# Attention and snake MLP on one core: the fourth chunk scaled by VectorE and transposed on TensorE, the fifth scaled in quarters, the last values interleaved, alpha spread later

## Chip, cores, metric

One core of a Trainium2 chip. The metric is the device time of one execution in microseconds (us). Every execution quoted is of the state "fast"; as will be seen, that state still holds several levels.

## The reference

```python
# q, k, v: (8, 12, 448, 64); w_in: (768, 2048); w_out: (2048, 768); float32
q_n, k_n = rmsnorm(q, g_q), rmsnorm(k, g_k)            # over the 64 of a head
attn = softmax(q_n @ k_n.T / 8)                         # per batch and head
x = (attn @ v), heads side by side                      # (3584, 768)
h = x @ w_in
g = h + sin(alpha * h)**2 / alpha
out = g @ w_out
```

## The kernel before

Eight batches, one after the other. Each has an attention stage and then its first product, h(b). The second product of a batch fills the gaps of the next batch's attention stage. In the first attention stage there is no such product, so TensorE runs dummy matmuls instead. q and k come in chunks of four heads, three chunks to a batch, numbered from 0: "fourth chunk" is number 3. Chunks 0 to 2 ("early") are scaled by VectorE (DVE) and transposed on TensorE (for chunk 1, 28 transposes of 64x64 take 0.89 us there, and the copies after them 1.16 us on DVE). The later ones are scaled by GpSimd (POOL) and transposed by DMA. Names in the profile: sc are scores, expT their exponentials, qkn scaled q and k, qkT the same transposed, av the values' products, hps the sums of h, g_sb the result of the snake function, osb the output before it is stored. What the change touches:

```python
def bank_pair(name, dtype=F32):          # PSUM: four pairs of banks; the pair expected
    slot = min(free_at, key=free_at.get) # to be free first is taken
    ...
early = ci < NC                          # NC = 3 chunks of a batch
def scale(w):
    eng = nc.vector if early else nc.gpsimd
    ...                                  # two multiplications of 128x448
def spread_alpha():                      # alpha to one column per tile
    ps = bank_pair("aps")
    nc.tensor.matmul(ps[:, 0, :MT], small, ident_f32, start=True, stop=True)
    nc.vector.tensor_copy(alpha_sb[:, :, 0], ps[:, 0, :MT])
    ...
# snake: who squares the sine
if m % 2 == 0 and (b or m <= MT // 2):
    nc.gpsimd.tensor_mul(s2, s1, s1)
else:
    nc.scalar.activation(s2, s1, ACT.Square)
...
# stage one: S_(n) is a tile of scores with n dummies ahead, A_ the values of a head pair
c0.pe_transpose((0, 1), (0,))
spread_alpha()
c1.reduce(0), c1.reduce(1)
S_(), S_()
c1.rsqrt()
S_(3)
c1.scale(0), c1.scale(1)
load_qk(NC)
S_(3), S_(2), S_(2), S_(1)
...                                      # chunks 1 and 2, loads of weights and v
A_(), S_(1), S_(1), S_(1)
c2.pe_transpose((0, 1))
S_(2), A_(), S_(2)
step_of(NC, 3, 4)()                      # chunk 3: sums of squares
S_(2), S_(1), A_()
step_of(NC, 5, 6)()                      # chunk 3: scale on GpSimd, DMA transposes, load chunk 6
load_w_out(1)
S_(1), S_(1), A_(), S_()
step_of(NC + 1, 3, 4)()
S_(), A_(2)                              # A_(2): pairs 4 and 5, key tiles 0 to 5, then tile 6
c4.rsqrt()                               # chunk 4: g folded, scaled and transposed beside h(0)
first_product(0, beside)
```

## Time and profile before

| | before |
|---|---|
| median of 3 runs | 439.59 us (438.88 to 439.76) |
| the profiled run, one more | 440.08 us, span 438.3 us |
| TensorE busy | 423.9 us (97%) |
| h(0) begins | 39.56 us |
| h(1) begins | 92.72 us |

The prediction shows the lines that carry the reading. After 83 us TensorE never waits, so as far as TensorE sets the time only the first 83 us can change it.

### The profile page before, as it was taken

To read this page: it belongs to the slowest core of one execution; us is meant where nothing else is said; L and a number is where in the kernel's file an instruction comes from. 1 tells how busy PE (TensorE), PEld (TensorE's weight loads), DVE (VectorE), ACT (ScalarE), POOL (GpSimd) and SP (SyncE) were. 2 spreads that over 40 slices of the span, in tenths; PEclk is the share of its full clock that TensorE was granted. 3 is DMA by queue.
4 is the path that set the end of the run, shared out by engine and by line. 5 is a ranking of instruction groups with operands and counts; after the bars stand their busy time and mean duration, and the time that the engine had idled before them with its cause. 6 is when DMAs were issued, how large, how long until landed. Compare 5 with 4: busy or idle time off the path is not lost.

```text
span 438.3 us, 9452 instructions
## 1 busy us (share of the span) xinstructions
PE 423.9 (97%) x3817; PEld 220.3 (50%) x3819; DVE 227.5 (52%) x329; ACT 340.0 (78%) x532; POOL 280.5 (64%) x264
## 2 busy tenths in 40 slices
PE   7889988999999999999999999999999999999996
PEld 3434543555555555555555554555555555555563
DVE  4767463547454574455636574555635474246511
ACT  5888897878888788878888788887878788788600
POOL 4969869917797469937699269956599276003300
PEclk9999999999999999999999999999999999999999
DMA  7999999790067804593076903596063901320022
GB/s 252 210 255 189 188 214 243 226 231 6 20 181 194 176 2 94 152 211 114 2 199 167 204 0 50 167 214 141 2 179 100 125 0 28 90 56 0 1 72 73
DMA packets 70096, 55.09 MB, mean 126 GB/s; under 512 B 41492, under 2 KB 65828, under 8 KB 70052
## 3 DMA queue, kind: packets, MB, share of 16 engines
q1 hardware_dynamic: 56690, 40.97, 36.9%
q0 software_dynamic: 12416, 11.81, 18.0%
q10 hardware_dynamic: 946, 1.70, 1.0%
q8 instruction: 30, 0.49, 0.4%
q14 instruction: 14, 0.11, 0.1%
HBM read 45.62 MB, written 11.01 MB: 129 GB/s over the span
## 4 chain that ended last, share of the span: by engine, by line
PE 83%; ACT 4%; DMA 4%; POOL 4%; DVE 2%; issue 2%; POOLq 0%; ACTq 0%
PE ops L400 31%; PE hps L353 30%; PE av L314 13%; PE sc L294 8%; DMA qkT<-qkn 3%; POOL qk L224 2%; ACT expT L297 2%; ACT s L332 1%; DMA qk<-in_k_dram 1%; POOL sq L221 1%; DVE ms L227 1%; DVE xT L326 1%; ACT s L337 1%; POOL vb L135 1%; DVE qkn L246 0%
## 5 line engine op out<-in xcount | busy, mean ns | idle before, releaser
L297 ACT ACTIVATE expT<-sc 128x896 bf16<-128x896 f32 x168 | 144.5, 912 | 31.9 <-PE sc L294 31.2
L400 PE MATMUL ops<-w_out_sb,g_sb 128*128 128x384 bf16 x896 | 156.7, 327 | 0.0
L353 PE MATMUL hps<-xT,w_in 128*128 128x448 bf16 x768 | 146.7, 353 | 0.0
L335 POOL TENSOR_TENSOR s<-s 128x448 f32<-128x448 f32 x61 | 56.7, 934 | 114.6 <-ACT s L332 100.4
L400 PEld LDWEIGHTS <-g_sb 128*128 128x128 bf16 x896 | 83.1, 98 | 69.5 <-issue 18.4
L340 DVE SCALAR_TENSOR_TENSOR g_sb<-s,inv_alpha_sb,hps 128x448 bf16<-128x448 f32 x128 | 80.8, 676 | 63.3 <-POOL s L335 62.3
L353 PEld LDWEIGHTS <-w_in 128*128 128x128 bf16 x768 | 74.5, 98 | 71.5 <-issue 2.9
L326 DVE TENSOR_TENSOR xT<-av,rec 64x448 bf16<-64x448 f32 x96 | 59.7, 622 | 70.6 <-ACT rec L321 51.5
L332 ACT ACTIVATE s<-hps,alpha_sb 128x448 f32<-128x448 f32 x128 | 74.9, 627 | 26.7 <-PE hps L353 23.9
L246 POOL TENSOR_TENSOR qkn<-qk,inv 128x448 bf16<-128x448 f32 x84 | 76.2, 940 | 10.0 <-POOL qk L224 6.0
L221 POOL TENSOR_TENSOR sq<-qk 128x896 f32<-128x896 f32 x44 | 73.4, 1686 | 0.0
L314 PE MATMUL av<-expT,vb 64*64 64x448 bf16 x672 | 69.2, 349 | 1.8 <-ACT expT L297 0.9
L314 PE MATMUL av<-expT,ones 64*64 64x448 bf16 x672 | 69.2, 349 | 0.0
L294 PE MATMUL sc<-qkT 64*64 64x448 bf16 x672 | 51.8, 361 | 4.4 <-DMA qkT<-qkn 1.8
L227 DVE TENSOR_REDUCE ms<-sq 128x14 f32<-128x896 f32 x44 | 46.8, 1081 | 16.3 <-POOL sq L221 16.1
L406 DVE COPY osb<-ops 128x768 f32<-128x768 f32 (+1 forms) x33 | 27.6, 837 | 46.7 <-PE ops L400 40.1
L224 POOL TENSOR_TENSOR qk<-qk,gg 128x896 f32<-128x896 f32 x24 | 50.2, 2091 | 1.8 <-ACT gg L171 1.7
L314 PEld LDWEIGHTS <-vb 64*64 64x64 bf16 x672 | 37.6, 107 | 14.0 <-issue 2.6
L314 PEld LDWEIGHTS <-ones 64*64 64x64 bf16 x672 | 37.1, 107 | 11.6
L337 ACT ACTIVATE s<-s 128x448 f32<-128x448 f32 x67 | 38.6, 577 | 3.5 <-DVE g_sb L340 0.5
L294 PEld LDWEIGHTS <-qkT 64*64 64x64 bf16 x672 | 15.3, 104 | 34.4 <-issue 28.5
L320 ACT ACTIVATE rec<-av 128x448 f32<-128x448 f32 x48 | 26.1, 544 | 3.7 <-PE av L314 3.2
(44 smaller groups left out, 136.6 us busy)
## 6 DMA issues: line engine op xcount, KB each, us to landing
qk<-in_q_dram SPq DMA_DIRECT2D x24, 448.0 KB, 5.5
qk<-in_k_dram SPq DMA_DIRECT2D x22, 448.0 KB, 5.9
out_dram<-osb SPq DMA_DIRECT2D x39, 192.0 KB, 2.8
vb<-in_v_dram POOLq DMA_DIRECT2D x32, 168.0 KB, 6.6
w_in<-in_moe_w_in_dram POOLq DMA_DIRECT2D x4, 768.0 KB, 11.0
w_out_sb<-in_moe_w_out_dram POOLq DMA_DIRECT2D x2, 1536.0 KB, 25.2
out_dram<-osb SPq DMA_DIRECT2D x26, 96.0 KB, 6.2
qk<-in_k_dram ACTq DMA_DIRECT2D x2, 448.0 KB, 6.0
```

The costliest lines, as they stand in the source:

```text
L221: nc.gpsimd.tensor_mul(st.sq[w], qk[ci][:, w], qk[ci][:, w])
L224: eng.tensor_mul(qk[ci][:, 0], qk[ci][:, 0], gg.to_broadcast([P, 2 * NJ, D]))
L246: eng.tensor_mul(n[:, :, hi, :], x[:, hi], inv[:, hi].unsqueeze(2).to_broadcast([P, NJ, D]))
L294: nc.tensor.matmul(sc[key_rows(pp, hi), pp, :S], qkt[r, 1, j * REST:(j + 1) * REST], qkt[r, 0, :], start=True, stop=True)
L297: nc.scalar.activation(expT[c, j], sc[:, :, :S], ACT.Exp, scale=SCALE)
L314: nc.tensor.matmul(av[o, part, :S], ones[r, :] if part else vb[b][r, hp, j, :], expT[pi // 2, j][r, pi % 2, :], start=(j == 0), stop=(j == ...
L326: nc.vector.tensor_mul(xT[b][r, hp, :], av[r, 0, :S], rec[o, :])
L332: nc.scalar.activation(s1, hps, ACT.Sin, scale=alpha_sb[:, m, :])
L335: nc.gpsimd.tensor_mul(s2, s1, s1)
L340: nc.vector.scalar_tensor_tensor(g_sb[:, m, (b % 2) * S:(b % 2 + 1) * S], s2, inv_alpha_sb[:, m, :], hps, op0=ALU.mult, op1=ALU.add)
L353: nc.tensor.matmul(ps[:, m % 2, :S], w_in_sb[m * 2 // MT][:, kt, m % (MT // 2) * P:(m % (MT // 2) + 1) * P], x[:, kt, :], start=(kt == 0), ...
L400: nc.tensor.matmul(st["ps"][:, k, :HALF], g_sb[:, m, c0:c0 + P], w_out_sb[:, m, half * HALF:(half + 1) * HALF], start=(m == 0), stop=(m == ...
```

## The change

Its intent: in the first stage GpSimd and the DMA queue are the late ones (chunk 4's transposes arrive near 72 us, and TensorE waits for them), while VectorE has time. So chunk 3 goes to VectorE and TensorE; chunk 4's folding of g moves up into the place set free on GpSimd; its scaling is cut in quarters between the squares of h(0), which all go to GpSimd; and the last two pairs' values are taken key tile by key tile, to use the wait for the last exponentials. Besides, alpha's matmul and copy move behind chunk 1's scaling, and chunk 6 and the second half of w_out are loaded earlier.

```diff
-        early = ci < NC
+        early = ci <= NC
-            for hi in range(2):
+            for hi in heads:                       # scale(w, heads=(0, 1))
...
-        if m % 2 == 0 and (b or m <= MT // 2):
+        if m % 2 == 0:
...
     c0.pe_transpose((0, 1), (0,))
-    spread_alpha()
...
-            for js in (range(NJ - 1), [NJ - 1]):
+            for j in range(NJ):
                 for pi in list(pairs)[:n]:
-                    attend(pi, js)
+                    attend(pi, [j])
...
     c1.scale(0), c1.scale(1)
+    spread_alpha()
     load_qk(NC)
...
+    load_w_out(1)
+    c4.fold_g()
     A_(), S_(1), S_(1), S_(1)
     c2.pe_transpose((0, 1))
-    S_(2), A_(), S_(2)
-    step_of(NC, 3, 4)()
-    S_(2), S_(1), A_()
-    step_of(NC, 5, 6)()
-    load_w_out(1)
+    S_()
+    c3.reduce(0), c3.reduce(1)
+    A_(), S_(2)
+    c3.rsqrt()
+    S_(2)
+    c3.scale(0), c3.scale(1)
+    load_qk(NC + 3)
+    S_(1), A_()
+    c3.pe_transpose((0, 1))
     S_(1), S_(1), A_(), S_()
...
-    for i, task in ((2, c4.fold_g), (4, lambda: c4.scale(0)), (5, lambda: c4.scale(1)), (6, step_of(NC + 1, 6))):
+    for i, task in ((2, lambda: c4.scale(0, [0])), (3, lambda: c4.scale(0, [1])), (4, lambda: c4.scale(1, [0])),
+                    (5, lambda: c4.scale(1, [1])), (6, step_of(NC + 1, 6)), (6, beside[3].pop())):
```

More of the change, by code (lines that the diff above doesn't have):

```diff
@@ L237, in rsqrt, with scale @@
             nc.scalar.activation(inv[:, ws, :2 * NJ], ln[:, ws], ACT.Exp, scale=-0.5)
-        def scale(w):
+        def scale(w, heads=(0, 1)):
             eng = nc.vector if early else nc.gpsimd
@@ L244, in scale @@
             inv = st.inv[w].rearrange("p (hi j) -> p hi j", hi=2)
-            for hi in range(2):
+            for hi in heads:
                 eng.tensor_mul(n[:, :, hi, :], x[:, hi], inv[:, hi].unsqueeze(2).to_broadcast([P, NJ, D]))
-            st.scaled += 1
-            if st.scaled == 2:
+            st.scaled += len(heads)
+            if st.scaled == 4:
                 for ps, time in st.inv_ps:
@@ L499 @@
     begin_norm(NC)
-    step_of(NC, 0, 1, 2)()
+    c3 = norm[NC]
+    c3.square(0), c3.square(1)
+    c3.fold_g()
     nc.gpsimd.tensor_copy(gate, qk[NC + 1][:, 1, 0, 0:1])
@@ L504 @@
     begin_norm(NC + 1)
-    step_of(NC + 1, 0, 1)()
+    c4 = norm[NC + 1]
+    c4.square(0), c4.square(1)
     for part in load_v(1):
         part()
+    load_w_out(1)
+    c4.fold_g()
     A_(), S_(1), S_(1), S_(1)
     c2.pe_transpose((0, 1))
-    S_(2), A_(), S_(2)
-    step_of(NC, 3, 4)()
-    S_(2), S_(1), A_()
-    step_of(NC, 5, 6)()
-    load_w_out(1)
+    S_()
[7 more added lines that the diff above has]
+    c3.pe_transpose((0, 1))
     S_(1), S_(1), A_(), S_()
-    step_of(NC + 1, 3, 4)()
+    c4.reduce(0), c4.reduce(1)
     S_(), A_(2)
-    c4 = norm[NC + 1]
     c4.rsqrt()
     beside = beside_h(0)
-    for i, task in ((2, c4.fold_g), (4, lambda: c4.scale(0)), (5, lambda: c4.scale(1)), (6, step_of(NC + 1, 6))):
+    for i, task in ((2, lambda: c4.scale(0, [0])), (3, lambda: c4.scale(0, [1])), (4, lambda: c4.scale(1, [0])),
+                    (5, lambda: c4.scale(1, [1])), (6, step_of(NC + 1, 6)), (6, beside[3].pop())):
         beside.setdefault(i, []).append(task)
```

## The prediction

> **What bounds the kernel now.** I read the busy strip first, then TensorE's waits in two windows, then the timelines of the first 95 us engine by engine. Three rows of the strip (40 slices of 11 us; tenths of busy time):
>
> ```profile
> PE   7889988999999999999999999999999999999996
> ACT  5888897878888788878888788887878788788600
> POOL 4969869917797469937699269956599276003300
> ```
>
> After the first eight slices TensorE is the bound. TensorE's waits say it exactly. From 0 to 40 us, and from 40 us to the end:
>
> ```profile
> PE sc L290 <- ACT expT L297: 1.2, 2, 1.1
> PE sc L294 <- DVE qkT L276: 1.0, 3, 0.7
> PE av L314 <- ACT expT L297: 0.9, 2, 0.7
> ...
> PE sc L294 <- DMA qkT<-qkn: 1.8, 2, 1.4
> PE sc L294 <- ACT expT L297: 1.0, 1, 1.0
> PE av L314 <- DVE osb L406: 0.9, 1, 0.9
> PE sc L294 <- DVE g_sb L340: 0.3, 1, 0.3
> ```
>
> The columns are total us, times, longest. The last four rows are all that TensorE loses after 40 us, 4.0 us of 398. TensorE's timeline gives their places, all between h(0) and the end of the second attention stage:
>
> ```profile
> 60.10 0.38 PE L294 MATMUL sc<-qkT 64*64 64x448 bf16 x4 [0.27 <-DVE g_sb L340]
> 63.88 0.38 PE L294 MATMUL sc<-qkT 64*64 64x448 bf16 x4 [1.03 <-ACT expT L297]
> 70.18 0.38 PE L294 MATMUL sc<-qkT 64*64 64x448 bf16 x2 [0.37 <-DMA qkT<-qkn]
> 71.97 0.76 PE L294 MATMUL sc<-qkT 64*64 64x448 bf16 x10 [1.41 <-DMA qkT<-qkn]
> 82.48 0.38 PE L314 MATMUL av<-expT,vb 64*64 64x448 bf16 x2 [0.90 <-DVE osb L406]
> ```
>
> From 83 us on it waits for nothing, so every microsecond won or lost before that point reaches the end unchanged, and nothing else can. The first stage (0 to 39.56 us, where h(0) starts) is different: TensorE there is padded with dummy matmuls and goes in step with ScalarE's exponentials, DVE and four PSUM bank pairs. ScalarE's and DVE's rows there:
>
> ```profile
> 14.58 0.32 ACT L236 ACTIVATE inv<-ms,eps 128x28 f32<-128x28 f32 x1
> 15.06 4.13 ACT L297 ACTIVATE expT<-sc 128x896 bf16<-128x896 f32 x5
> 20.04 2.53 ACT L297 ACTIVATE expT<-sc 128x896 bf16<-128x896 f32 x3 [0.85 <-PE sc L294]
> 15.22 2.22 DVE L246 TENSOR_TENSOR qkn<-qk,inv 128x448 bf16<-128x448 f32 x4 [0.67 <-POOL gate L444]
> 18.41 1.16 DVE L276 COPY qkT<-tp 128x896 bf16<-128x896 bf16 x2 [0.98 <-PE tp L269]
> ```
>
> An exponential costs 0.82 us of pitch, a DVE scaling of a chunk 2.22, a copy of a transposed chunk 1.16. ScalarE stands still for only 2.4 us between 27 and 40 us, so delays before that cannot be made up.
>
> [...] the wait at 82.48 is for an osb copy that stood behind two reductions on DVE (79.36 to 81.44). [...] a tile in a pair keeps the next one out until it is read. The trace shows such waits (60.10, 82.48). [...] Here 28 of 64x64 take 0.89 us on TensorE and 1.16 us on DVE. [...] chunk 4's transposes are issued at 58.84 behind chunk 6's load, issued at 48.30 and about 13 to 15 us in landing, and end near 72.
>
> **The change, part by part.** I followed the order of instructions that the build gives, and the bank pair that each tile gets, with durations from the trace. S1 to S21 are the score tiles of stage one, e1 to e21 their exponentials, A the value products of a head pair.
>
> *Alpha later.* The alpha matmul's bank pair is now taken between S3 and S4, and is freed by a DVE copy that stands behind chunk 1's scaling. S5 gets that same pair. The reductions come 0.4 us sooner, so the scaling ends near 17.2 (15.0 plus 2.2) and the alpha copy at 17.35; S5 starts there, not at 14.93. S5 to S7 with their dummies take 2.35 us, transposes and copies bring S8 to 21.3, and e8 to about 22.3 instead of 20.04: +2.2. S14 loses its two dummies (0.5), so e14 comes near 29.3 instead of 27.64: +1.7.
>
> *Chunk 3 on DVE and TensorE.* Its Ln and Exp (0.5) move ahead of e16, with no net cost. The scaling runs on DVE after pair 1's xT, 33.4 to 35.6; the transposes (0.89) stand ahead of S18 on TensorE and wait for it, so e18 comes near 36.95 instead of 34.12: +2.8. Pair 3's A gets the bank pair of the transposes, freed by DVE's copies, which stand behind pair 2's xT: 37.3 to 38.5. So A starts at 38.5, its rec ends at 41.1, e20 runs 41.1 to 42.0, and the delay is +4.3 (before: 36.78).
>
> *Last values by key tile.* Meant to use the wait for e20. But pair 5's accumulator gets the bank pair that S20 held, free only after e20. In the new order its first product is second in the queue, so 13 of 14 steps of 0.19 us wait until 42.05, where before 5 of pair 4 had gone ahead (9 were left at 37.73). The end is 42.05 + 2.47 = 44.5, so h(0) starts near 44.6: +5.0.
>
> *h(0).* The fifth chunk's g is folded earlier, so POOL has 8 squares, 4 quarters and 2 squares of chunk 5: 8 x 0.93 + 4 x 0.91 + 2 x 1.68 = 14.4 us in 18.2. ScalarE loses three squares of 0.58. Its last one ends 19.5 us after h(0) begins, not 22.05, and the last g 21.3 after, not 22.8. The waits at 60.10 and 63.88 (0.27 + 1.03) vanish.
>
> *Chunk 4's transposes.* Quarters end some 16.5 us into h(0), transposes are issued near 61.1, and S8 of stage two needs them near 73.5. Chunk 6's load now leaves near 35.6 and chunk 3's DMA transposes are gone, so 12.4 us are left for what took 11.75 to 13 us behind a load. The waits of 0.37 + 1.41 go: with the two above, -3.1.
>
> *The wait at 82.48* follows DVE's order, which is unchanged there; I take 0.2 off it.
>
> Sum: 5.0 - 3.1 - 0.2 = +1.7; 439.6 + 1.7 gives 441.3 us.
>
> **Rivals.** (a) The change works as meant: stage one is no longer than before and the 3.1 us, plus the wait of 0.7 us at A, come out: 435.8. For it: the waits removed are real, and the DMA queue has slack. Against it: S5 waits for DVE, and pair 5 for e20, in the built order, which no duration can undo. (b) Only half of the delay of stage one survives, because ScalarE's idle time (2.4 us after 27 us) takes some of it: +2.5 - 3.1, so 439.0. Against it: this idle time is mostly used in my count, and the new stalls (transposes behind the scaling, A behind the copies) come after it. (c) Chunk 4's transposes still land late, since the second half of w_out is issued earlier and shares the engines, or POOL falls behind with its quarters: 1 to 2 us of the 3.1 come back, 442.8. Against it: the start of h(0) is itself later, and the DMA work is less. (d) xT of pairs 4 and 5 comes too late for h(0)'s last key tile, as rec and c4's reductions stand before it: +0.5. By my count it is ready at 48.15, needed at 48.4.
>
> **Range and chances.** Stage one: +3.8 to +5.8; from h(0) on: -2.2 to -4.0. The corners give -0.2 to +3.6, or 439.4 to 443.2; (b) and further slips on that side are more likely than their mirrors, so the lower end is taken a microsecond further down: 438.4 to 443.2. Two per cent is 8.8 us, more than the whole of the waits on either side: same 0.96, faster 0.02, slower 0.02.
>
> **What would show it.** Right if the timeline shows S5 waiting on DVE until about 17.4, e8 near 22.3, a wait of about 1 us on DVE ahead of pair 3's A and one of over 1 us on e20 in the last A, the first hps matmul near 44.6, no wait on the qkT transposes nor on the exponential at the start of stage two, and still none after 90 us. Wrong if h(0) begins before 43 us (then the time is below 439.8), if waits on qkT return, or if later stages lose TensorE time.

## The result

442.81 us median of 4 runs (442.41 to 444.31), against 439.42 (438.88 to 439.76; the three runs above and a fourth). The ratio is 1.0084, 95% interval 1.0058 to 1.0111: 0.8% slower, inside the class "same". (A ratio here is the mean time of one kernel's fast runs over the mean of the other's of the same rounds, so not quite the ratio of the medians.)

TensorE's waits in the changed kernel, from 0 to 46 us and from 46 us to the end (total us, times, longest):

```profile
PE sc L290 <- DVE alpha_sb L178: 1.7, 1, 1.7
PE av L314 <- ACT expT L297: 1.5, 1, 1.5
...
PE av L314 <- DVE qkT L276: 1.0, 1, 1.0
PE tp L269 <- DVE qkn L246: 0.9, 2, 0.5
...
PE av L314 <- DVE osb L406: 0.9, 1, 0.9
PE sc L294 <- ACT expT L297: 0.3, 1, 0.3
```

The first four are new or longer and stand in stage one; of the waits after it, 4.0 us in four rows before, 1.2 us are left, and none on qkT. Their places in TensorE's timeline of the changed kernel:

```profile
17.45 0.59 PE L290 MATMUL sc<-blank 128*128 128x512 bf16 x2 [1.70 <-DVE alpha_sb L178]
...
40.49 0.38 PE L314 MATMUL av<-expT,vb 64*64 64x448 bf16 x2 [1.04 <-DVE qkT L276]
...
44.06 0.38 PE L314 MATMUL av<-expT,vb 64*64 64x448 bf16 x2 [1.49 <-ACT expT L297]
...
46.65 18.34 PE L353 MATMUL hps<-xT,w_in 128*128 128x448 bf16 x96
...
72.36 0.57 PE L294 MATMUL sc<-qkT 64*64 64x448 bf16 x8 [0.32 <-ACT expT L297]
```

These are S5 waiting for the alpha copy, pair 3's values waiting for DVE's copies of chunk 3's transposes, and the last values waiting for e20. h(0) begins at 46.65 us, 7.1 later than before. h(1) begins at 96.02, 3.3 later: 3.8 us are won in between. From there TensorE stays 3.3 us behind to its end, but the last transfer out is shorter: the span ends 3.9 us after the start of VectorE's last copy (437.31), where it was 4.3 before (434.01). So the span grows by 2.9 us. That "nothing else can" change the time, as the prediction says, is off by these 0.4 us; no run looked for their cause.

All these waits were forecast, but h(0) was forecast at 44.6. The other 2 us are, as E2 will show, in the clock. Busy time per stretch of 3 us, first of the changed kernel, then of the one before; the last three columns are granted TensorE clock (1.00 is full), DMA share and GB/s:

```profile
16.00:19.00 3.00, 1.55 (x12) 0.43 (x11) 1.65 (x5) 1.31 (x2) 3.00 (x3) 1.00 1.15 259
19.00:22.00 3.00, 2.73 (x37) 1.54 (x33) 0.23 (x1) 2.15 (x3) 2.46 (x2) 0.50 1.13 225
22.00:25.00 3.00, 2.55 (x10) 0.60 (x10) 2.91 (x4) 1.24 (x2) 1.00 (x1) 0.50 1.10 257
25.00:28.00 3.00, 3.00 (x39) 1.24 (x38) 0.83 (x2) 2.68 (x6) 3.00 (x3) 0.86 1.10 259
```

```profile
16.00:19.00 3.00, 2.36 (x39) 1.19 (x38) 2.02 (x5) 3.00 (x4) 3.00 (x2) 1.00 1.18 218
19.00:22.00 3.00, 2.75 (x34) 1.32 (x38) 2.56 (x4) 2.15 (x4) 3.00 (x3) 1.00 1.08 211
```

After a stretch in which TensorE worked only 1.55 of 3 us (the wait at S5), its clock is halved for about 6.8 us (3 + 3 + 0.8; read in windows of 0.2 us, from 19.0 to 25.8). In the profiled executions of E1, E3, E4, F1 and of the third session below it is halved once, for 3.4 us (F1's also reads 0.90 from 14 to 17 us). A "window" of the clock is, in what follows, such a stretch of 3.4 us at half clock; the 6.8 us count as two. Chunk 1's 28 transposes take 1.46 us there, 0.89 before. After which stretches the clock fell and after which it did not is in the last section; why it falls no run shows.

### The profile page after: what moved, and what is told of

Read it like the earlier page. It is cut to its first block, busy times and chain, and to the rows that moved or that the text cites. A ratio compares the mean times of both kernels' runs of the same rounds, so it can differ in the third digit from the quotient of the medians.

```text
span 441.2 us, 9507 instructions
## 1 busy us (share of the span) xinstructions
PE 425.9 (97%) x3842; PEld 221.7 (50%) x3845; DVE 230.9 (52%) x335; ACT 339.2 (77%) x529; POOL 279.5 (63%) x263
## 4 chain that ended last, share of the span: by engine, by line
PE 80%; ACT 2%; DVE 2%; issue 0%
PE ops L400 32%; PE hps L353 29%; PE av L314 12%; PE sc L294 7%; ACT expT L297 1%; DVE ms L227 1%; DVE osb L406 0%; DVE g_sb L340 0%; DVE xT L326 0%; ACT rec L321 0%; ACT inv L236 0%; ACT inv L237 0%; ACT rec L320 0%
## 5 line engine op out<-in xcount | busy, mean ns | idle before, releaser
L335 POOL TENSOR_TENSOR s<-s 128x448 f32<-128x448 f32 x64 | 59.4, 932 | 121.7 <-ACT s L332 108.2
L246 POOL TENSOR_TENSOR qkn<-qk,inv 128x448 bf16<-128x448 f32 x80 | 72.6, 937 | 7.4 <-POOL qk L224 7.0
L337 ACT ACTIVATE s<-s 128x448 f32<-128x448 f32 x64 | 36.9, 577 | 2.8
```

The source lines that it names most:

```text
L246: eng.tensor_mul(n[:, :, hi, :], x[:, hi], inv[:, hi].unsqueeze(2).to_broadcast([P, NJ, D]))
```

## The experiments

Eleven runs in three sessions, each session on another chip. The median of the kernel before was 439.13 us in the first session (42 runs), 439.24 in the second (28) and 439.07 in the third (19); its quickest execution took 438.16, 437.98 and 437.75. All kernels gave correct results.

| kernel | median (range) us, runs | ratio, 95% interval | h(0) begins in the profiled run |
|---|---|---|---|
| changed | 442.81 (442.41 to 444.31), 4 | 1.0084 (1.0058 to 1.0111) | 46.65 |
| changed, second session | 442.49 (441.15 to 442.78), 6 | 1.0070 (1.0046 to 1.0093) | 46.37 |
| changed, third session | 441.73 (440.91 to 444.25), 6 | 1.0071 (1.0046 to 1.0097) | 46.00 |
| E1 alpha early | 440.17 (438.82 to 441.49), 14 | 1.0020 (1.0007 to 1.0033) | 44.06 |
| E2 dummies at alpha | 442.55 (441.14 to 445.22), 6 | 1.0083 (1.0059 to 1.0108) | 44.83 |
| E2 again | 442.42 (441.19 to 445.21), 6 | 1.0091 (1.0064 to 1.0117) | 44.81 |
| E3 old order of pairs | 441.64 (440.05 to 445.09), 13 | 1.0062 (1.0042 to 1.0083) | 45.30 |
| E4 squares alone, on the kernel before | 440.18 (438.63 to 441.94), 22 | 1.0026 (1.0016 to 1.0037) | 39.69 |
| F1 = E1 + E3 | 439.36 (438.02 to 440.78), 14 | 1.0003 (0.9985 to 1.0021) | 43.00 |
| F2 = F1 + transposes in h(0) | 436.36 (436.24 to 437.73), 7 | 0.9947 (0.9925 to 0.9969) | 38.98 |
| G1 = F1 + chunk 3 on GpSimd and DMA | 439.93 (437.54 to 442.53), 14 | 1.0021 (0.9999 to 1.0042) | 38.98 |
| H1 = F2 with the new order of pairs | 437.34 (437.02 to 438.50), 14 | 0.9973 (0.9961 to 0.9985) | 41.18 |

Each run reports its mean clock, and the runs stand in steps. E1, for example: six runs at a clock of 0.998 to 1.000 took 438.82 to 439.01 us; of the eight at 0.994 to 0.996, five took 440.14 to 440.40 and three 441.23 to 441.49. So one halved window costs about 1.3 us there, and a slow start costs about as much (S1 at 13.35 us instead of 12.0, below); the three at 441.2 to 441.5 may have had both, but none of them was profiled. The cost depends on where the window falls: E3 has an execution at 0.996 that took 440.19, no longer than its four at 1.000 (440.05 to 440.40). Kernels are therefore compared by their lowest step as well as by the median.

**E1, alpha back at its old place.**

```diff
     c0.pe_transpose((0, 1), (0,))
+    spread_alpha()
...
     c1.scale(0), c1.scale(1)
-    spread_alpha()
```

> The changed kernel with alpha's matmul and DVE copy back at their old place, ahead of the first scores. Theory: S5 no longer waits for DVE, TensorE's clock stays at full speed, e14 comes near 27.2 us instead of 31.2, h(0) begins near 42.7 instead of 46.65, and the time falls by about 4 us to 438.8. Rival (chunk 3's scaling and transposes make the whole delay of stage one, alpha is harmless): h(0) stays near 46.5 and the time at 442.8.

The lowest step is 438.8 to 439.0, as the theory said, 2.2 us under the changed kernel's own lowest step (441.0). The median gained 2.6. In the profiled run h(0) came at 44.06 and not at 42.7, because the clock fell all the same, later, after chunk 3's stalls (the granted clock is the third column from the end):

```profile
33.00:36.00 3.00, 2.11 (x37) 1.02 (x33) 2.40 (x5) 2.06 (x4) 3.00 (x3) 1.00 1.00 168
36.00:39.00 3.00, 2.42 (x28) 1.29 (x32) 0.53 (x1) 0.68 (x1) 3.00 (x6) 0.52 1.07 209
```

So alpha's new place costs 2.2 us at equal clock. That the clock would then stay up was wrong.

**E2, the wait at S5 filled with dummies.** The alpha copy stays where the change put it.

```diff
-    spread_alpha()
+    aps = bank_pair("aps")
+    nc.tensor.matmul(aps[:, 0, :MT], small, ident_f32, start=True, stop=True)
...
-    S_(3), S_(2), S_(2), S_(1)
+    S_(3)
+    for _ in range(7):
+        nc.tensor.matmul(aps[:, 1], blank[:, :P], blank, start=True, stop=True)
+    nc.vector.tensor_copy(alpha_sb[:, :, 0], aps[:, 0, :MT])
...
+    S_(2), S_(2), S_(1)
```

> The changed kernel with alpha where it put it, but with 7 dummy matmuls in the spare bank of alpha's pair, so that TensorE works while S5 waits. Theory (the wait costs about 2 us by itself, and the half clock after it another 2): S5 still begins near 17.5, the clock is 1.00 from 19 to 26 us, h(0) begins near 44.6, time about 440.8. Rival (the half clock costs nothing, as the stage is bound by ScalarE and DVE): clock 1.00 but h(0) still near 46.5, time 442.8.

TensorE's timeline of this run:

```profile
17.46 0.59 PE L290 MATMUL sc<-blank 128*128 128x512 bf16 x2 [0.27 <-DVE alpha_sb L496]
...
44.83 18.33 PE L353 MATMUL hps<-xT,w_in 128*128 128x448 bf16 x96
```

S5 begins at the same time as in the changed kernel, the clock stays at 1.00 (read from 13 to 25 us), and h(0) begins at 44.83, not 46.65: the 1.8 us are what the two halved windows cost in that first profiled run. The time of that execution was 441.17. But the median did not move (442.55): four of the six executions lost their clock all the same (means of 0.992 to 0.996).

**E3, the old order of the last pairs.**

```diff
-            for j in range(NJ):
+            for js in (range(NJ - 1), [NJ - 1]):
                 for pi in list(pairs)[:n]:
-                    attend(pi, [j])
+                    attend(pi, js)
```

> The changed kernel with the last values in the old order, pair 4's first six key tiles ahead of pair 5's. Theory (pair 5's bank pair is free only after e20, so the new order holds pair 4 back): five steps of pair 4 run ahead of the wait, h(0) begins near 45.9 instead of 46.65, time about 442.0. Rival (the new order works as meant): h(0) near 47.3, time 443.4.

In TensorE's timeline the wait at the last values is 0.74 us (1.49 in the changed kernel). Its h(0), at 45.30, is not to be set against the forecast, as this execution lost one window (17.1 to 20.5 us). Two more comparisons at equal clock agree: the lowest steps of E2 and E3, which differ by this order and the dummies, are 441.15 and 440.05 to 440.40; those of E1 and F1, of two sessions, are 438.9 and 438.05. The new order costs about 0.8 us.

**E4, one line of the change alone, on the kernel before.**

```diff
-        if m % 2 == 0 and (b or m <= MT // 2):
+        if m % 2 == 0:
```

> The kernel before with one line of the change: h(0)'s even squares all on GpSimd. Theory (chunk 4's transposes land near 72 us whatever ScalarE does): the waits of 0.3 and 1.0 us at 60 and 64 us vanish, the wait on qkT grows by as much, time unchanged at 439.4. Rival (each wait removed is won): 437.9.

The time was not better (ratio 1.0026), but not for the reason expected. TensorE's timeline shows one new long wait, and the one on qkT is gone:

```profile
62.09 0.38 PE L294 MATMUL sc<-qkT 64*64 64x448 bf16 x4 [2.12 <-DVE g_sb L340]
...
69.39 0.38 PE L294 MATMUL sc<-qkT 64*64 64x448 bf16 x4 [0.22 <-DVE osb L406]
```

g_sb waits for squares: with chunk 4's folding (2.09 us) still beside h(0), GpSimd cannot take three more squares, and works without a break from 46.4 to 63.7 us. The scores then come late enough to find qkT there. And the clock falls again: in this execution it is halved from 63.5 to 66.9 us, right after the new wait (the 12 matmuls of the second product from 62.40 on take 3.00 us, 2.12 in the kernel before), and 17 of the 22 executions have a mean clock of 0.996 or less. The five others took 438.6 to 439.9 us, close to the kernel before (438.2 to 439.6), so the slower median is in large part this lost window. Alone, the squares bring nothing; what they bring beside the rest of the change no run isolates.

**The changed kernel again,** for its spread:

> The changed kernel unaltered, for its spread. Theory [...]: nearly every run has a mean clock of 0.996 or less, and the times stand in steps of about 1.3 us, 442.5 for one slow window and more for two or three; a run at 1.000, if there is one, would be near 441.1. Rival (the clock is noise): times don't go with the clock.

One of six stood at 441.15. Only three had a mean clock of 0.996 or less, where nearly all were expected, and two others had a mean of 1.000 and took 442.5 and 442.7, so the clock's mean is not all. The profiled one of those (442.7; span 440.9) shows why: its group of 15 dummies ahead of S1 took 5.11 us against 3.41 in the kernel before, and S1 began at 13.35 us instead of 12.0. The clock column says 1.00 there all the same. The slow start is read from the dummies alone: 0.40 to 0.44 us each in the first group of both kernels, 0.23 in the second group of the kernel before, 0.34 here. Whether it is the clock no view shows; the mean of 1.000 does not show it.

**F1, alpha early and the old order together:**

> The changed kernel with alpha early and the pairs in the old order. Theory (the parts add): at full clock 438.9 of the first experiment less 0.8, so 438.1, h(0) beginning near 41.9 us; runs with a slow window 1.3 us more. Rival (ScalarE's e21 sets the end in either order once alpha is early): 438.8 at full clock.

At full clock 438.02 to 438.24, as forecast: the two parts add. It only equals the kernel before, as the stalls at chunk 3's transposes and the falls of the clock behind them remain.

**F2, chunk 3's transposes moved into h(0).**

```diff
-    c3.pe_transpose((0, 1))
     S_(1), S_(1), A_(), S_()
...
-    for i, task in ((2, lambda: c4.scale(0, [0])), ...
+    for i, task in ((3, lambda: c3.pe_transpose((0, 1))), (2, lambda: c4.scale(0, [0])), ...
```

> As the one before, and chunk 3's transposes moved out of stage one into h(0), beside its fourth pair of tiles. Theory (the stalls at the transposes and at pair 3's values, 0.4 and 1.05 us and what follows, come from where the transposes stand): h(0) begins near 39.3 and is 0.9 us longer, no wait on qkT, time 435.8, faster than both kernels, and no slow window. Rival (moving chunk 3 to DVE delays stage one by itself, through the scaling): h(0) not before 41, time 437.5.

436.36 us, ratio 0.9947 (0.9925 to 0.9969): 0.5% faster than the kernel before, and the best found; quickest against quickest it is 1.7 us (436.24 and 437.98). "No slow window" was wrong: two of the seven executions lost one, and a third stood at 437.7 with a mean clock of 1.000. TensorE's timeline:

```profile
37.15 0.38 PE L314 MATMUL av<-expT,vb 64*64 64x448 bf16 x2 [0.71 <-ACT expT L297]
38.98 9.25 PE L353 MATMUL hps<-xT,w_in 128*128 128x448 bf16 x48
48.98 9.25 PE L353 MATMUL hps<-xT,w_in 128*128 128x448 bf16 x48
```

h(0) begins at 38.98, is cut in two by the transposes and is 0.9 us longer (10.0 us from one half's start to the next's; 9.1 in the other kernels), and nothing waits for qkT after it. From S1 to h(0) it takes 27.2 us, and 26.8 in G1 (next), where GpSimd scales chunk 3. So scaling chunk 3 on VectorE cost stage one 0.3 us at most; where its transposes stood cost more.

**G1, as F1, but chunk 3 on GpSimd and DMA as before.** (Edit: `early = ci < NC` again; `c3.transpose()` after `c3.scale`, then the load of chunk 6, the second half of w_out and chunk 4's fold.)

> The changed kernel with alpha early, the pairs in the old order, and chunk 3 scaled on GpSimd and transposed by DMA as before; the fifth chunk's early fold and quarters stay. Theory (the gain from h(0) on needs chunk 3 off GpSimd and off the DMA queue, so that chunk 6's load leaves early): h(0) near 39.3, but the wait on qkT at the eighth score tile of stage two stays, 1 to 2 us, and the time is 438 to 439.3. Rival (the gain comes from the fold and the quarters alone): no wait on qkT, 435.5.

TensorE's timeline of this run:

```profile
68.89 0.38 PE L294 MATMUL sc<-qkT 64*64 64x448 bf16 x2 [0.98 <-DMA qkT<-qkn]
...
71.03 0.75 PE L294 MATMUL sc<-qkT 64*64 64x448 bf16 x10 [1.76 <-DMA qkT<-qkn]
```

h(0) begins at 38.98 as in F2, but the wait on qkT is back, 2.7 us of it. The median of 439.93 lies above the forecast 438 to 439.3, which four of the five executions with a mean clock of 1.000 fit (438.2 to 439.5). So fold and quarters alone do not bring the gain after h(0): it needs chunk 3 off GpSimd and the DMA queue. Which of the two, the DMA queue's timelines show, of G1 and then of F2 (DMA_TRANSPOSE: chunk 3 at 42.35, chunk 4 at 56; qk<-in_q: chunk 6's load):

```profile
42.35 5.08 SPq L256 DMA_TRANSPOSE qkT<-qkn  x2
47.54 0.52 SPq L122 DMA_DIRECT2D qk<-in_q_dram  x1
...
56.18 7.57 SPq L256 DMA_TRANSPOSE qkT<-qkn  x2
```

```profile
33.18 0.37 SPq L122 DMA_DIRECT2D qk<-in_q_dram  x1
...
56.35 4.47 SPq L256 DMA_TRANSPOSE qkT<-qkn  x2
```

GpSimd is done with chunk 4 at the same time in both. But F2's transposes land 8.2 to 8.8 us after their issue, while G1's are waited for until 71.03, 14.9 us after the first was issued. So GpSimd's own time for chunk 4 is not it, the DMA side is: the load of chunk 6, which in G1 comes behind chunk 3's transposes and with them waits for GpSimd, stands shortly ahead of chunk 4's transposes. (GpSimd also asks for the second half of w_out 3.8 us later in G1, at 42.27; its share no run separates.) In the changed kernel the load leaves at 37.50 (48.30 before), and chunk 4's transposes land in 3.5 to 3.9 us.

**The changed kernel a third time,** for the share of executions that lose their clock:

> The changed kernel again, for the share of its executions in which TensorE's clock is halved, beside the next one on the same chip. So far 1 of 10 stood at 441.2 and the rest at 442.3 to 444.3. Theory: again at most one in five at 441.2.

Three of six stood at 440.9 to 441.1, more than expected; over the three sessions it is 4 of 16. The profiled execution is worth reading, because its clock was full until 38.5 us. TensorE's timeline:

```profile
17.32 0.59 PE L290 MATMUL sc<-blank 128*128 128x512 bf16 x2 [1.70 <-DVE alpha_sb L178]
21.25 0.38 PE L294 MATMUL sc<-qkT 64*64 64x448 bf16 x2 [0.72 <-DVE qkT L276]
...
38.52 0.58 PE L314 MATMUL av<-expT,vb 64*64 64x448 bf16 x2 [1.05 <-DVE qkT L276]
...
46.00 18.33 PE L353 MATMUL hps<-xT,w_in 128*128 128x448 bf16 x96
```

Forecast were 17.35 for S5, 21.3 for S8 and 38.5 for pair 3's values. In ScalarE's timeline e8, e14 and e18 begin at 22.20, 29.27 and 36.90; forecast were 22.3, 29.3 and 36.95. Then the clock falls for one window (0.91 from 36 to 39 us, 0.52 from 39 to 42), and h(0) comes at 46.0 instead of 44.6.

**E2 a second time:**

> The kernel with 7 dummy matmuls in alpha's spare bank again. Theory (the idle stretch at S5 is what lets the clock fall there): clearly more executions at 441.2 than the unaltered changed kernel beside it, 1 in 3 or more; those that still fall do so later, at the stalls of chunk 3. Rival (the clock falls elsewhere, whatever happens at S5): the same share.

One of six at 441.2. With the first time it is 3 of 12, beside 4 of 16 of the changed kernel, and a mean clock of 0.996 or less stands in 9 of 12, beside 9 of 16. So filling the wait at S5 did not make the fall rarer, as far as so few executions tell, and the theory that this wait is what decides it fell. Whether a stall lets the clock down in a given execution, which one, and how often, stays open.

**H1, F2 with the new order of the pairs.** (F2 without E3's edit.)

> The version with alpha early and chunk 3's transposes in h(0), but the last values interleaved by key tile, as the change has them. Theory (pair 5's bank pair comes free only after e20): h(0) begins 0.8 us later than the 38.98 of the old order, time 437.1. Rival (interleaving helps once nothing else delays e20): 435.9.

437.34 us against F2's 436.36; lowest steps 437.0 to 437.3 and 436.2 to 436.4. TensorE's timeline has the wait at the last values twice as long as F2's 0.71:

```profile
38.59 0.38 PE L314 MATMUL av<-expT,vb 64*64 64x448 bf16 x2 [1.47 <-ACT expT L297]
```

(This execution started slowly, as in the second session above: 5.25 us for the 15 dummies, 13.17 us for S1, so its h(0) at 41.18 is not to be set against 38.98. From S1 to h(0) it takes 28.0 us, F2 27.2.) The order costs 0.8 to 1.0 us here too, so the rival falls.

## Why the prediction was right, point by point

The direction and the place of each term were right, and the measured median, 442.8, lies in the range, 1.5 us above the sum's 441.3. The delay was 3.4 us (3.3 and 2.7 in the later sessions) where 1.7 was forecast. The sum was made for a clock at full speed; the four quickest of the changed kernel's 16 executions, all with a mean clock of 1.000, took 440.9 to 441.2. None of these was profiled, but from h(0) to the end all three profiled executions take 394.5 to 394.6 us, so with spans of 439.1 to 439.4 they began h(0) near 44.6 to 44.8, an estimate that fits the forecast 44.6.

That 441.3 was met so well is in part luck. The sum was worked out on an execution of 440.08 us but set on the median, 439.6, half a microsecond lower; and after h(0) 3.8 + 0.4 us were won, 0.9 more than the 3.3 forecast. Against that profiled execution the account closes: 440.1 + 5.1 - 3.8 - 0.4 gives 441.0. But the kernel before has quicker executions too, and quickest against quickest the change cost 3.2 us in the second and in the third session. What those quicker executions save no profile shows.

- *Alpha later, +2.2 at e8.* In the execution with full clock S5 and S8 came within 0.05 us of the forecast. E1 puts the cost of the place at 2.2 us at the lowest step. (From the changed kernel over E1 and F1 to F2 the lowest step falls by 2.2, 0.8 and 1.8 us.)
- *Chunk 3: stalls at its transposes and at pair 3's values.* Both were there (0.42 and 1.05 us). F2 against F1 gives their cost: 1.8 us at the lowest step (438.05 less 436.25), in spite of the 0.9 us that the transposes add to h(0) there.
- *Last values by key tile.* Forecast as a loss (2.47 us left after e20 instead of 1.71). E3, F1 and H1 all give 0.8 to 1.0 us.
- *h(0) at 44.6.* It came at 46.65, 46.37 and 46.00 in the three profiled executions. The first and the third had the half clock ahead of h(0) (from 19.0 to 25.8 and from 38.5 to 41.9 us), the second a slow start (5.11 us for the 15 dummies). E2's profiled executions, with a full clock, had it at 44.83 and 44.81, and the way there is the forecast one: in the first of them pair 3's values at 38.66 (38.5), e20 at 41.29 (41.1), the end of the last wait at 42.24 (42.05). The term that was missing from the sum is this half clock, worth about 1.3 us for one halved window and 1.8 for the two of the first profiled execution, or a slow start, and nothing in my working had either.
- *From h(0) on, -3.1, and -0.2 at the osb copy.* The four waits went, as said, a new one of 0.3 us came, and the wait for the osb copy stayed at 0.89, so the waits alone fell by 2.8. The gain between h(0) and h(1) was 3.8. The rest is in the spacing of the score tiles: two in a row with no wait between take 0.5 us with the start of what follows, and with a wait between 0.2 more than that wait (the stretch from the first pair of tiles to the second: 3.02 us before, 2.56 after, of which 0.27 was the wait). So these waits cost more than their length. For chunk 4's transposes the forecast had 12.4 us left, for what had taken 11.75 to 13; they took 3.5 to 3.9, so the margin was far larger than thought.
- *Rivals.* (a), all as meant, fell for this kernel, but F2 at 436.4 is near what it promised (435.8), once alpha, the order and the transposes stand elsewhere. (b) fell: ScalarE's idle time took nothing back. (c) fell: no wait on qkT; that its 442.8 is the measured median is chance. (d) did not show.

## What to carry to other kernels

Moving work to an idle engine can be free while the buffer it uses is not: here the losses came from PSUM pairs that were given back late, by DVE copies that stood behind other work of DVE (alpha's at 17.23 us behind 2.21 us of scaling, chunk 3's at 39.28 behind 1.26 us of xT) or by the last exponentials (pair 5's, a wait of 1.49 us), and this can be read from the built order and the pairs before anything runs. In a stage like this first one, count a new stall twice, once for itself (alpha's place: 2.2 us) and once for the half clock that may follow it (here about 1.3 us for one window, 1.8 for two). And give such a kernel many executions: its time stands in steps, and a median of four can be off by a step.

## Where TensorE's clock fell, and where it did not

- It fell after stretches that were only partly idle: 1.55 of 3 us busy (16 to 19 us), with a longest wait of 1.70 us, in the changed kernel; 1.70 of 3 (36 to 39 us, the fall at 38.5 within them) in its third session; 2.11 of 3 (33 to 36 us) in E1. It did not always: 1.68 of 3 us (16 to 19 us) in the third session and 1.12 of 3 (16 to 19 us) in the second passed at full clock. A share of busy time at which it falls cannot be read from these runs.
- For changes of less than 1% the start counts: between two executions the group of 15 dummies ahead of S1 took 3.41 or 5.11 us, and S1 came at 12.0 or 13.35.
- 28 transposes of 64x64 took 0.89 us at full clock (32 ns each) and 1.46 at half clock (52 ns each).
